# Attention feeding two expert layers on one core: the low-part subtractions issued on VectorE, and the decay and mask products given 64 rows

## The chip, the cores and the metric

The kernel runs on one core of a Trainium2 chip. The metric is device time in microseconds (us). The engines are named as in the profile: PE is TensorE's matrix multiply and PEld its weight load, DVE is VectorE, ACT is ScalarE, POOL is GpSimd, and SP is SyncE, which issues most of the DMAs. Each engine takes its instructions in the order in which they are written in its own stream, and waits where a semaphore isn't there yet.

## The reference, cut to what matters

Attention over 4 batches, 8 heads, 576 positions and a head size of 64, with a decay from cumulated logarithms of `f` and a causal mask; its output goes through a dense layer with a squared ReLU, and that through 8 experts of which each token takes two.

```python
scores = scale * np.matmul(q, k.transpose(0, 1, 3, 2))
cum = np.cumsum(np.log(np.clip(f, 0.0001, 1.0)), axis=-1)
decay = cum[:, :, :, None] - cum[:, :, None, :]
scores = np.where(causal, -1000000000.0, scores + decay)
attn = softmax(scores)                 # over the last axis
x = np.matmul(attn, v)                 # then (2304 tokens, 512)
h = np.maximum(x @ w_in, 0.0); x = h * h @ w_out
# then two of eight experts for each token, weighted
```

## The kernel before, in words

All products run on pairs of float16 numbers: a value is kept as a high part (a cast on ACT) and a low part (the value less the high part), and a product is three matmuls, high by high, high by low and low by high. So each split is one ACT instruction, then one subtraction that reads two tensors in SBUF. Most of those subtractions in the attention are on POOL: `prep` (L163, queries and keys of a pair of heads), `att_split` (L241 and L252, the probabilities), `att_out` (L302, the attention's output), `hd_prep` from the second batch on (L327) and `hd_split` (L381).

The scores of two heads, z = 0 and 1, lie on the lower and the upper 64 rows of the array: the three products at L187 (query tiles of 128), L200 (the last tile, 64 queries, both heads in one bank) and L349 (`hd_s`) use tiles of 64 rows. To these a decay product is added: the 24 rows of `crow` hold the cumulated logarithms of 8 heads in three parts, and `esel` picks a head's three rows, at L190, L201 and L354 with 24 rows. Last comes the mask, as a product of a unit matrix and a triangle: 128 rows at L192 and L358, 64 rows at L204. DVE takes the row maximum (L217, L366), ACT the exponential (L220, L227, L371), then the split, a DMA transpose issued by SP, and the product with the values (L282, L285, L398).

The first 256 positions of every batch ("heads", `hd_*`, 12 units) come first, and beside them DVE and ACT turn the first weights into high and low parts (`conv_w`: L434, L435, L436 and L444 on DVE, 32 times in all). Then the first expert layer runs in passes of chunks of 384 tokens: `mm1` (L456), its squared ReLU on ACT and DVE (L460, L461, then L464 in chunks 0 and 1, and L466 with L467 in later ones), and `mm2` (L500) two steps behind. Chunks 0 and 1 are done in two passes each. The remaining attention (48 units: 3 query tiles of 4 batches, 4 pairs of heads) is issued between the steps of the passes, and a scheduler in the framework sets the final order on every engine from its own cost model. After the last attention come chunk 5 and the second layer's experts (L740, L753), which the change doesn't touch.

Of the kernel before, what the change touches and what calls it, by code (L numbers as in the profile page):

```python
# [52 lines left out]
def attn_moe_moe_kernel(ctx: ExitStack, tc, qka, qk, v, f, w_io, wgn, noise, w1, w2, out):  # L53
# [53 lines left out]

    identb = consts.tile([128, 128], BF16, name="identb")
    masku = consts.tile([128, 128], BF16, name="masku")
    esel = apool.tile([128, H, 128], F16, name="esel")  # L110
    crow = apool.tile([128, B, S], F16, name="crow")
    nc.gpsimd.memset(identb, 0.0)
    nc.gpsimd.affine_select(identb, identb, [[-1, 128]], ALU.not_equal, 1.0, base=0, channel_multiplier=1)
    nc.gpsimd.memset(masku, 0.0)
    nc.gpsimd.affine_select(masku, masku, [[-1, 128]], ALU.is_ge, -BIG, base=0, channel_multiplier=1)

# [22 lines left out]
    for z in range(2):  # L139
        es = esel[64 * z:64 * z + 24]  # L140
        nc.gpsimd.memset(es, -8.0)
        nc.gpsimd.affine_select(es, es, [[-3, 8], [0, 128]], ALU.is_ge, 0.0, base=0, channel_multiplier=1)
        nc.gpsimd.affine_select(es, es, [[3, 8], [0, 128]], ALU.is_ge, 0.0, base=2, channel_multiplier=-1)
    ident2k = consts.tile([128, 128], F16, name="ident2k")
# [12 lines left out]
    def prep(b, p):  # L157
        n = p
        if b == 0:
            make_set(n)  # L160
        t = raw.pop(("qk", b, p))
        nc.scalar.activation(QK[n][:, 0], t, AF.Copy)
        nc.gpsimd.tensor_tensor(QK[n][:, 1], t, QK[n][:, 0], op=ALU.subtract)  # L163

# [12 lines left out]
    def att_s(u, pools):  # L177
# [4 lines left out]
        if i < 4:  # L182
# [5 lines left out]
            for z in range(2):  # L188
                r = slice(64 * z, 64 * z + 24)
                nc.tensor.matmul(st[u][z][:, :N], esel[r, 2 * p + z], crow[r, b, :N], start=False, stop=False)  # L190
            for z in range(2):
                nc.tensor.matmul(st[u][z][:, N - 128:N], identb, masku, start=False, stop=True)  # L192
        else:
            for hf in range(2):
                ps = st[u][hf]
                ks = slice(288 * hf, 288 * hf + 288)
                for x, (qi, ki) in enumerate(HL3):
                    for z in range(2):
                        r = slice(64 * z, 64 * z + 64)
                        nc.tensor.matmul(ps[r, :288], QK[n][r, qi, q0:q0 + 64], QK[n][r, ki, ks], start=(x == 0), stop=False, skip_group_check=True)  # L200
                nc.tensor.matmul(ps[:, :288], esel.rearrange("r h t -> r (h t)")[0:24, 256 * p + 64:256 * p + 192], crow[0:24, b, ks], start=False, stop=(hf == 0), skip_group_check=True)  # L201
            for z in range(2):
                r = slice(64 * z, 64 * z + 64)
                nc.tensor.matmul(st[u][1][r, 224:288], identb[r, 64 * z:64 * z + 64], masku[r, 64 * z:64 * z + 64],  # L204
                                 start=False, stop=True, skip_group_check=True)

# [24 lines left out]
    def att_split(u):  # L231
        b, i, p = u
        pr, = st[u]
        if i < 4:
            phl = astream.tile([128, 4, 2, 2, 128], F16, name="phl", bufs=3)
            pt = astream.tile([128, 4, 2, 2, 128], F16, name="pt", bufs=3)
            for h in range(2):
                pv = pr[:, h, :128 * (i + 1)].rearrange("p (k s) -> p k s", s=128)
                hi, lo = phl[:, :i + 1, h, 0, :], phl[:, :i + 1, h, 1, :]
                nc.scalar.activation(hi, pv, AF.Copy)  # L240
                nc.gpsimd.tensor_tensor(lo, pv, hi, op=ALU.subtract)  # L241
            nc.sync.dma_start_transpose(out=pt[:, :i + 1].rearrange("p a b c q -> p (a b c) q"),
                                        in_=phl[:, :i + 1].rearrange("p a b c s -> p (a b c s)"))
        else:
# [4 lines left out]
            for k0, k1, w_ in ((0, 4, 128), (4, 5, 64)):  # L249
                s3 = flat[:, 128 * k0:128 * k0 + w_ * (k1 - k0)].rearrange("p (k s) -> p k s", s=w_)  # L250
                nc.scalar.activation(ph4[:, k0:k1, 0, :w_], s3, AF.Copy)
                nc.gpsimd.tensor_tensor(ph4[:, k0:k1, 1, :w_], s3, ph4[:, k0:k1, 0, :w_], op=ALU.subtract)  # L252
            nc.sync.dma_start_transpose(out=pt.rearrange("p a b q -> p (a b) q"),
# [39 lines left out]
    def att_out(b, i, po, su, su_in):  # L293
# [7 lines left out]
        nc.scalar.activation(xh[:, 0], xs[:, :, :n], AF.Copy)  # L301
        nc.gpsimd.tensor_tensor(xh[:, 1], xs[:, :, :n], xh[:, 0], op=ALU.subtract)  # L302
        t0 = HEAD * b + 128 * i if i < NB else NTH + REST * b + 128 * (i - NB)
# [17 lines left out]
    def hd_prep(b):  # L321
        for x in range(2):
# [3 lines left out]
            nc.scalar.activation(s_[:, 0], t, AF.Copy)  # L326
            (nc.vector if b == 0 else nc.gpsimd).tensor_tensor(s_[:, 1], t, s_[:, 0], op=ALU.subtract)  # L327

# [8 lines left out]
    def hd_s(u, bank):  # L337
# [13 lines left out]
        for p in range(np_):  # L351
            for z in range(2):
                r = slice(64 * z, 64 * z + 24)
                nc.tensor.matmul(ps[z][:, W * p:W * p + W], esel[r, 2 * (np_ * a + p) + z], crow[r, b, 0:W],  # L354
                                 start=False, stop=False, skip_group_check=True)
        v4 = [t.rearrange("p (c w) -> p c w", w=W) for t in ps]
        for z in range(2):
            nc.tensor.matmul(v4[z][:, :, 128 * i:128 * i + 128], identb, masku[:, None, :].to_broadcast([128, np_, 128]),  # L358
                             start=False, stop=True, skip_group_check=True)
        if a == 0:  # L360
# [14 lines left out]
    def hd_split(u):  # L375
# [4 lines left out]
        nc.scalar.activation(phl[:, 0], flat, AF.Copy)  # L380
        nc.gpsimd.tensor_tensor(phl[:, 1], flat, phl[:, 0], op=ALU.subtract)  # L381
        nc.sync.dma_start_transpose(out=pt, in_=phl.rearrange("p a s -> p (a s)"))
# [646 lines left out]
```

## Time and profile before

| what | value |
|---|---|
| three runs | 1086.57, 1088.98 (median), 1092.2 us |
| the profiled execution | 1083.63 us, of which 1081.9 us are its span |
| busy of the span | PE 991.0, DVE 579.6, ACT 443.3, POOL 369.3 us |
| mean granted TensorE clock | 0.986 |

A share of busy time is an average over stages; below, the stages are taken apart. An instruction's length includes what it waits for inside itself, such as a memory port.

### The profile page before, as it was taken

The numbers are of one execution on the slowest core, as the hardware profiler recorded it, in microseconds if no ns is written. First come the engines' busy times: TensorE is split into PE (matmuls) and PEld (weight loads), VectorE is DVE, ScalarE is ACT, GpSimd is POOL, SyncE is SP. The second block draws the span as 40 slices with busy tenths as digits, with TensorE's granted clock in tenths as the row PEclk, the third lists the DMA queues.
The fourth block names the chain that finished last, engine by engine and source line by source line (L and its number), as shares of the span: only waits on it lengthen the run. The fifth ranks groups of instructions, "written<-read, shape, count | busy, mean of one in ns | idle before, by whom it ended". The sixth has DMA issues, their size and how long they took to land.

```text
span 1081.9 us, 18041 instructions
## 1 busy us (share of the span) xinstructions
PE 991.0 (92%) x7050; PEld 537.5 (50%) x7050; DVE 579.6 (54%) x1159; ACT 443.3 (41%) x989; POOL 369.3 (34%) x331
## 2 busy tenths in 40 slices
PE   3748898899999999999998989998999999999996
PEld 1425444455454554555454434446646474646563
DVE  8998899624766666665537614214734343433121
ACT  3756676644555554564336312003513131412020
POOL 7454632311546535623410230533232404030202
PEclk9999899999999999999999989999999999999999
DMA  7599999433766784672529462437995938370303
GB/s 275 162 201 194 264 224 232 104 76 77 146 141 145 186 176 86 135 144 36 93 40 311 156 155 59 69 69 153 322 214 160 210 93 214 97 148 10 49 1 50
DMA packets 240393, 153.50 MB, mean 142 GB/s; under 512 B 194066, under 2 KB 204626, under 8 KB 240306
## 3 DMA queue, kind: packets, MB, share of 16 engines
q1 hardware_dynamic: 230194, 131.32, 50.3%
q0 software_dynamic: 10112, 21.02, 10.4%
q8 instruction: 56, 0.92, 0.4%
q14 instruction: 31, 0.25, 0.1%
HBM read 81.63 MB, written 24.30 MB: 98 GB/s over the span
## 4 chain that ended last, share of the span: by engine, by line
PE 62%; DVE 16%; DMA 9%; issue 6%; ACT 3%; POOL 2%; SPq 1%; ACTq 0%; POOLq 0%; DVEq 0%
PE e L753 18%; PE e L740 16%; PE m L456 10%; PE acc L500 9%; DMA wr<-in_w_dram 3%; DMA w<-in_w_io_dram 2%; DVE w L435 2%; PE ps L187 2%; DVE w L436 1%; DVE w L434 1%; PE po L282 1%; DVE r L466 1%; DVE wout L444 1%; DVE sm L217 1%; PE ps L200 1%
## 5 line engine op out<-in xcount | busy, mean ns | idle before, releaser
L740 PE MATMUL e<-xgT,w1s 128*128 128x320 f16 (+2 forms) x1536 | 217.8, 302 | 7.1 <-DMA xgT<-xg 5.0
L456 PE MATMUL m<-xT,win 128*128 128x384 f16 x1152 | 209.7, 332 | 13.7 <-ACT r L460 13.1
L500 PE MATMUL acc<-wout,g 128*128 128x512 f16 x864 | 205.6, 380 | 11.2 <-DVE g L464 6.3
L753 PE MATMUL e<-w2s,hT 128*128 128x512 f16 x960 | 212.1, 380 | 3.9 <-ACT hT L744 3.9
L740 PEld LDWEIGHTS <-w1s 128*128 128x128 f16 x1536 | 143.5, 99 | 80.7 <-issue 13.7
L456 PEld LDWEIGHTS <-win 128*128 128x128 f16 x1152 | 110.0, 99 | 88.8 <-issue 23.3
L753 PEld LDWEIGHTS <-hT 128*128 128x128 f16 x960 | 93.7, 98 | 114.0 <-ACT hT L744 4.2
L500 PEld LDWEIGHTS <-g 128*128 128x128 f16 x864 | 81.8, 98 | 102.2 <-DVE g L464 10.8
L744 ACT ACTIVATE hT<-e 128x320 f16<-128x320 f32 (+2 forms) x128 | 53.9, 435 | 186.3 <-PE e L740 186.2
L757 POOL DMA_INDIRECT out_dram<-y,tix x40 | 63.9, 1598 | 142.9 <-DVE y L756 134.7
L745 DVE SCALAR_TENSOR_TENSOR hT<-e,hT 128x320 f16<-128x320 f32 (+2 forms) x128 | 60.4, 487 | 96.0 <-ACT hT L744 95.8
L756 DVE TENSOR_SCALAR y<-e,gs 128x512 f32<-128x512 f32 x40 | 30.0, 750 | 146.0 <-PE e L753 131.6
L466 DVE TENSOR_TENSOR r<-r 128x384 f32<-128x384 f32 x64 | 56.8, 888 | 90.7 <-ACT g L461 90.7
L241 POOL TENSOR_TENSOR phl<-pr,phl 128x384 f16<-128x384 f32 (+1 forms) x64 | 68.7, 1090 | 81.6 <-issue 59.8
L460 ACT ACTIVATE r<-m 128x384 f32<-128x384 f32 x96 | 46.6, 486 | 90.9 <-PE m L456 85.4
L706 POOL DMA_INDIRECT xg<-x2d,tix x40 | 44.7, 1117 | 113.4 <-DMA xgT<-xg 103.5
L641 POOL DMA_INDIRECT table<-ent,si x36 | 36.1, 1002 | 127.8 <-DVE si L638 99.0
L676 ACT ACTIVATE w2s<-wr 128x1024 f16<-128x1024 f32 x32 | 32.5, 1050 | 106.3 <-PE e L753 88.5
L217 DVE TENSOR_REDUCE sm<-ps 128x1 f32<-128x384 f32 (+2 forms) x96 | 51.7, 561 | 34.0 <-PE ps L192 20.8
L220 ACT ACTIVATE pr<-ps,sm 128x384 f32<-128x384 f32 (+1 forms) x64 | 40.0, 627 | 57.7 <-DVE sm L219 56.1
L349 PE MATMUL psab<-hs 64*128 64x128 f16 (+1 forms) x192 | 27.7, 342 | 26.2 <-ACT pr L371 14.7
L461 ACT ACTIVATE g<-r 128x384 f16<-128x384 f32 x96 | 50.2, 522 | 1.8
(253 smaller groups left out, 1160.0 us busy)
## 6 DMA issues: line engine op xcount, KB each, us to landing
wr<-in_w_dram SPq DMA_DIRECT2D x64, 512.0 KB
w<-in_w_io_dram SPq DMA_DIRECT2D x32, 512.0 KB
qkr<-in_qk_dram SPq DMA_DIRECT2D x16, 448.0 KB
vr<-in_v_dram SPq DMA_DIRECT2D x16, 320.0 KB
x2d<-x SPq DMA_DIRECT2D x18, 256.0 KB
qkh<-in_qka_dram SPq DMA_DIRECT2D x8, 512.0 KB
out_dram<-zero SPq DMA_DIRECT2D x5, 768.0 KB
vh<-in_v_dram SPq DMA_DIRECT2D x8, 256.0 KB
```

The lines of the kernel that those rows point to most:

```text
L217: seen[u] = nc.vector.tensor_reduce(sm[:, z:z + 1], ps[z][:, :N], AX.X, ALU.max).ins
L241: nc.gpsimd.tensor_tensor(lo, pv, hi, op=ALU.subtract)
L456: nc.tensor.matmul(ps, win[i][:, cc, wi, :], xT[:, xi, cc, r0:r0 + CH], start=(x == 0), stop=(x == 11))
L460: nc.scalar.activation(r, ps, AF.Relu)
L461: nc.scalar.activation(g[:, 0, :], r, AF.Square, scale=2.0 ** -10)
L466: nc.vector.tensor_tensor(r, r, r, op=ALU.mult)
L500: nc.tensor.matmul(acc[t], g[:, gi, 128 * t:128 * t + 128], wout[i][:, wi, :], start=(i in ends[c][0] and x == 0), stop=(i in ends[c][1] a ...
L740: nc.tensor.matmul(ps[:, :hw], w1s[:, cc, wi, 128 * i:128 * i + 128], xgT[:, 4 * xi + cc, hw * q:hw * q + hw], start=(x == 0), stop=(x == 11))
L744: nc.scalar.activation(hi, ps[:, :hw], AF.Relu)
L745: nc.vector.scalar_tensor_tensor(hT[:, i, 1, hw * q:hw * q + hw], ps[:, :hw], 0.0, hi, op0=ALU.max, op1=ALU.subtract)
L753: nc.tensor.matmul(ps, hT[:, i, hi, 128 * j:128 * j + 128], w2s[:, i, wi, :], start=(i == 0 and x == 0), stop=(i == NFE - 1 and x == 2))
L757: s_ = nc.gpsimd.indirect_dma_start(out=out, out_offset=bass.IndirectOffsetOnAxis(ap=tix[:, j, 0:1], axis=0), in_=y, in_offset=None, compu ...
```

## The change

Every one of those subtractions is issued on DVE. `crow` is cleared on POOL and `esel` shrinks to one number a row and head, of which 64 rows are set; `decay` spreads it over the columns of the weight load by a step of zero. The decay product then takes 64 rows, and in the last tile it is two products, one for each head, in place of one. The mask of 128 rows becomes two halves of 64 rows for each head. Line numbers of the changed kernel are larger: L435 is L447, L444 is L456, L466 is L478, L467 is L479, L464 is L476.

```diff
-    identb = consts.tile([128, 128], BF16, name="identb")
-    masku = consts.tile([128, 128], BF16, name="masku")
-    esel = apool.tile([128, H, 128], F16, name="esel")
+    identb = consts.tile([128, 2, 128], BF16, name="identb")
+    masku = consts.tile([128, 2, 128], BF16, name="masku")
+    esel = apool.tile([128, H], F16, name="esel")
     crow = apool.tile([128, B, S], F16, name="crow")
+    nc.gpsimd.memset(crow, 0.0)
     nc.gpsimd.memset(identb, 0.0)
-    nc.gpsimd.affine_select(identb, identb, [[-1, 128]], ALU.not_equal, 1.0, base=0, channel_multiplier=1)
     nc.gpsimd.memset(masku, 0.0)
-    nc.gpsimd.affine_select(masku, masku, [[-1, 128]], ALU.is_ge, -BIG, base=0, channel_multiplier=1)
+    for z in range(2):
+        for t_, cmp, val in ((identb, ALU.not_equal, 1.0), (masku, ALU.is_ge, -BIG)):
+            t_ = t_[64 * z:64 * z + 64]
+            nc.gpsimd.affine_select(t_, t_, [[64, 2], [-1, 128]], cmp, val, base=0, channel_multiplier=1)
...
     for z in range(2):
-        es = esel[64 * z:64 * z + 24]
+        es = esel[64 * z:64 * z + 64]
         nc.gpsimd.memset(es, -8.0)
-        nc.gpsimd.affine_select(es, es, [[-3, 8], [0, 128]], ALU.is_ge, 0.0, base=0, channel_multiplier=1)
-        nc.gpsimd.affine_select(es, es, [[3, 8], [0, 128]], ALU.is_ge, 0.0, base=2, channel_multiplier=-1)
+        nc.gpsimd.affine_select(es, es, [[-3, 8]], ALU.is_ge, 0.0, base=0, channel_multiplier=1)
+        nc.gpsimd.affine_select(es, es, [[3, 8]], ALU.is_ge, 0.0, base=2, channel_multiplier=-1)
+
+    def decay(r, h, m):
+        return esel[r, h:h + 1].to_broadcast([64, m])
+
...
-        nc.gpsimd.tensor_tensor(QK[n][:, 1], t, QK[n][:, 0], op=ALU.subtract)
+        nc.vector.tensor_tensor(QK[n][:, 1], t, QK[n][:, 0], op=ALU.subtract)
...
             for z in range(2):
-                r = slice(64 * z, 64 * z + 24)
-                nc.tensor.matmul(st[u][z][:, :N], esel[r, 2 * p + z], crow[r, b, :N], start=False, stop=False)
-            for z in range(2):
-                nc.tensor.matmul(st[u][z][:, N - 128:N], identb, masku, start=False, stop=True)
+                r = slice(64 * z, 64 * z + 64)
+                nc.tensor.matmul(st[u][z][:, :N], decay(r, 2 * p + z, 128), crow[r, b, :N], start=False, stop=False)
+            for hf in range(2):
+                for z in range(2):
+                    r = slice(64 * z, 64 * z + 64)
+                    nc.tensor.matmul(st[u][z][:, N - 128:N], identb[r, hf], masku[r, hf], start=False, stop=(hf == 1))
...
-                nc.tensor.matmul(ps[:, :288], esel.rearrange("r h t -> r (h t)")[0:24, 256 * p + 64:256 * p + 192], crow[0:24, b, ks], start=False, stop=(hf == 0), skip_group_check=True)
+                for z in range(2):
+                    r = slice(64 * z, 64 * z + 64)
+                    nc.tensor.matmul(ps[r, :288], decay(r, 2 * p + z, 64), crow[r, b, ks], start=False, stop=(hf == 0), skip_group_check=True)
...
-                nc.gpsimd.tensor_tensor(lo, pv, hi, op=ALU.subtract)
+                nc.vector.tensor_tensor(lo, pv, hi, op=ALU.subtract)
...
-        nc.gpsimd.tensor_tensor(xh[:, 1], xs[:, :, :n], xh[:, 0], op=ALU.subtract)
+        nc.vector.tensor_tensor(xh[:, 1], xs[:, :, :n], xh[:, 0], op=ALU.subtract)
...
-            (nc.vector if b == 0 else nc.gpsimd).tensor_tensor(s_[:, 1], t, s_[:, 0], op=ALU.subtract)
+            nc.vector.tensor_tensor(s_[:, 1], t, s_[:, 0], op=ALU.subtract)
...
-        nc.gpsimd.tensor_tensor(phl[:, 1], flat, phl[:, 0], op=ALU.subtract)
+        nc.vector.tensor_tensor(phl[:, 1], flat, phl[:, 0], op=ALU.subtract)
```

The scheduler's order changes with it. The first place is PE's stream at the end of a last-tile unit in the chunk-2 pass: three products (the last is shown; `set` holds queries and keys), the decay (`esel`, `crow`), the mask (`identb`, `masku`), and then values times probabilities (`pt`). Before:

```order
L200 LDWEIGHTS set_1571
L200 MATMUL ps<-set_1571 64x288
L201 LDWEIGHTS esel
L201 MATMUL ps<-crow,esel 128x288
L204 LDWEIGHTS identb
L204 MATMUL ps<-masku,identb 64x64
L204 LDWEIGHTS identb
L204 MATMUL ps<-masku,identb 64x64
L282 LDWEIGHTS pt
L282 MATMUL po<-vs,pt 128x64
```

The changed kernel, the same unit:

```order
L209 LDWEIGHTS set_1602
L209 MATMUL ps<-set_1602 64x288
L212 LDWEIGHTS esel
L212 MATMUL ps<-crow,esel 64x288
L212 LDWEIGHTS esel
L212 MATMUL ps<-crow,esel 64x288
L215 LDWEIGHTS identb
L215 MATMUL ps<-masku,identb 64x64
L215 LDWEIGHTS identb
L215 MATMUL ps<-masku,identb 64x64
L292 LDWEIGHTS pt
L292 MATMUL po<-vs,pt 128x64
```

Between the products of scores and those of the mask stands a pair of 64-row decay products where one of 24 rows stood.

The second place is DVE's stream in the heads: the weight conversion (L434 to L444, in the changed kernel L446 to L456), the row maxima and their scaling (`smh`), and the subtractions. Before:

```order
L434 TENSOR_SCALAR w_371<-w_361 128x512
L295 TENSOR_SCALAR sums<-sums 128x8
L435 SCALAR_TENSOR_TENSOR w_371<-w_361,w_371 128x512
L296 RECIPROCAL sums<-sums 128x8
L366 TENSOR_REDUCE smh<-psab 128x2
L436 SCALAR_TENSOR_TENSOR w_361<-w_361,w_371 128x512
L367 TENSOR_SCALAR smh<-smh 128x2x2
L444 SCALAR_TENSOR_TENSOR win_148<-w_311,win_148 128x4x128
L366 TENSOR_REDUCE smh<-psab 128x4
L444 SCALAR_TENSOR_TENSOR wout_164<-w_313,wout_164 128x512
L366 TENSOR_REDUCE smh<-psab 128x4
```

The changed kernel:

```order
L446 TENSOR_SCALAR w_494<-w_376 128x512
L379 TENSOR_SCALAR smh<-smh 128x2x2
L447 SCALAR_TENSOR_TENSOR w_494<-w_376,w_494 128x512
L456 SCALAR_TENSOR_TENSOR wout_171<-w_324,wout_171 128x512
L448 SCALAR_TENSOR_TENSOR w_376<-w_376,w_494 128x512
L393 TENSOR_TENSOR phlh<-pr,phlh 128x1024
L378 TENSOR_REDUCE smh<-psab 128x4
L337 TENSOR_TENSOR hs<-qkh,hs 128x1024 x2
L456 SCALAR_TENSOR_TENSOR win_156<-w_374,win_156 128x4x128
L378 TENSOR_REDUCE smh<-psab 128x4
L446 TENSOR_SCALAR w_500<-w_490 128x512
L393 TENSOR_TENSOR phlh<-pr,phlh 128x1024
```

The subtractions of the probabilities (`phlh`) and of the next batch's queries and keys (`hs`) now stand between the conversions and the maxima. Up to the fifteenth `g` of chunks 0 and 1 (L464, L476), 30 of the 32 conversions stand ahead in the kernel before and 26 in the changed one.

The third place is DVE's stream around the eighth and ninth step of chunk 2: the squared ReLU (`r`, `g`), the maxima and the split of the probabilities (`phl`). Before:

```order
L217 TENSOR_REDUCE sm<-ps 128x1
L219 TENSOR_SCALAR sm<-sm 128x1
L217 TENSOR_REDUCE sm<-ps 128x1
L466 TENSOR_TENSOR r<-r 128x384
L219 TENSOR_SCALAR sm<-sm 128x1
L467 SCALAR_TENSOR_TENSOR g<-r,g 128x384
L217 TENSOR_REDUCE sm<-ps 128x1 x2
L219 TENSOR_SCALAR sm<-sm 128x1 x2
L295 TENSOR_SCALAR sums<-sums 128x8
L296 RECIPROCAL sums<-sums 128x8
L466 TENSOR_TENSOR r<-r 128x384
L467 SCALAR_TENSOR_TENSOR g<-r,g 128x384
```

The changed kernel:

```order
L251 TENSOR_TENSOR phl<-pr,phl 128x4x128
L229 TENSOR_SCALAR sm<-sm 128x1
L227 TENSOR_REDUCE sm<-ps 128x1
L478 TENSOR_TENSOR r<-r 128x384
L229 TENSOR_SCALAR sm<-sm 128x1
L251 TENSOR_TENSOR phl<-pr,phl 128x4x128
L479 SCALAR_TENSOR_TENSOR g<-r,g 128x384
L305 TENSOR_SCALAR sums<-sums 128x8
L306 RECIPROCAL sums<-sums 128x8
L251 TENSOR_TENSOR phl<-pr,phl 128x4x128 x2
L478 TENSOR_TENSOR r<-r 128x384
L479 SCALAR_TENSOR_TENSOR g<-r,g 128x384
```

Three subtractions of the probabilities have come between one `r` and the next.

## Rows read from the trace of the kernel before

**Rows 1.** Windows of four stretches: start:end, length, busy us (instructions) of PE, PEld, DVE, ACT, POOL.

```profile
0.00:216.00 216.00, 160.74 (x1187) 85.81 (x1188) 186.22 (x285) 132.84 (x329) 103.56 (x82) 0.98 0.83 207
216.00:279.00 63.00, 63.00 (x488) 32.86 (x485) 22.94 (x79) 30.60 (x69) 14.90 (x15) 1.00 0.31 72
279.00:568.00 289.00, 279.75 (x2472) 146.78 (x2471) 174.59 (x424) 145.50 (x356) 126.38 (x131) 0.99 0.58 123
568.00:1082.00 514.00, 487.47 (x2910) 272.02 (x2909) 195.87 (x373) 134.32 (x235) 124.48 (x104) 0.98 0.57 134
```

**Rows 2.** Timeline of PE, 341 to 347 us: start, length, line, tiles, shape, count.

```profile
343.30 0.56 PE L200 MATMUL ps<-set 64*64 64x288 f16 x6
343.79 0.29 PE L201 MATMUL ps<-crow,esel 24*128 24x288 f16 x1
344.01 0.55 PE L200 MATMUL ps<-set 64*64 64x288 f16 x6
...
344.87 0.87 PE L282 MATMUL po<-vs,pt 128*128 128x64 f16 x24
```

**Rows 3.** Groups of DVE, 0 to 216 us: count, busy us, mean ns, idle before.

```profile
L435 DVE SCALAR_TENSOR_TENSOR w<-w,w 128x512 int32<-128x512 int32 x32 | 29.7, 927 | 0.4
L436 DVE SCALAR_TENSOR_TENSOR w<-w,w 128x512 int32<-128x512 int32 x32 | 27.9, 871 | 0.4
L444 DVE SCALAR_TENSOR_TENSOR wout<-w,wout 128x512 f16<-128x512 f32 x16 | 21.7, 1354 | 2.1 <-ACT wout L443 1.9
L434 DVE TENSOR_SCALAR w<-w 128x512 int32<-128x512 int32 x32 | 20.6, 643 | 6.7 <-DMA w<-in_w_io_dram 6.5
L444 DVE SCALAR_TENSOR_TENSOR win<-w,win 128x512 f16<-128x512 f32 x16 | 15.9, 995 | 0.8 <-ACT win L443 0.7
L464 DVE TENSOR_TENSOR g<-r,g 128x384 f16<-128x384 f32 x20 | 14.8, 739 | 7.1 <-ACT r L463 7.1
```

**Rows 4.** Single lines on DVE, whole run: shortest, median, longest in ns.

```profile
L435 DVE SCALAR_TENSOR_TENSOR w<-w,w x32: 642/692/2494, 14.9 to 194.7; 128x512 int32<-128x512 int32 x32
L444 DVE SCALAR_TENSOR_TENSOR wout<-w,wout x16: 678/685/2617, 24.8 to 198.2; 128x512 f16<-128x512 f32 x16
L434 DVE TENSOR_SCALAR w<-w x32: 408/426/2336, 14.3 to 193.8; 128x512 int32<-128x512 int32 x32
L466 DVE TENSOR_TENSOR r<-r x64: 546/558/5471, 288.5 to 644.9; 128x384 f32<-128x384 f32 x64
```

**Rows 5.** Groups of POOL, 0 to 216 us, the subtractions.

```profile
L381 POOL TENSOR_TENSOR phlh<-pr,phlh 128x1024 f16<-128x1024 f32 x12 | 27.4, 2288 | 45.9 <-ACT phlh L380 34.5 <-issue 11.3
L327 POOL TENSOR_TENSOR hs<-qkh,hs 128x1024 f16<-128x1024 f32 x6 | 14.7, 2471 | 0.1
L302 POOL TENSOR_TENSOR xh<-xs,xh 128x512 f16<-128x512 f32 x9 | 13.2, 1470 | 20.5 <-ACT xh L301 20.4
L163 POOL TENSOR_TENSOR set<-qkr,set 128x896 f16<-128x896 f32 x5 | 10.8, 2164 | 0.3 <-ACT set L162 0.2
L241 POOL TENSOR_TENSOR phl<-pr,phl 128x512 f16<-128x512 f32 x8 | 10.1, 1277 | 27.6 <-issue 23.6 <-ACT phl L240 4.0
L241 POOL TENSOR_TENSOR phl<-pr,phl 128x384 f16<-128x384 f32 x8 | 8.6, 1077 | 8.0 <-ACT phl L240 5.4 <-issue 1.8 <-POOL phl L241 0.8
```

**Rows 6.** The same subtraction where it already ran on DVE, whole run.

```profile
L327 DVE TENSOR_TENSOR hs<-qkh,hs x2: 1207/1207/1207, 9.0 to 10.9; 128x1024 f16<-128x1024 f32 x2
```

**Rows 7.** Timeline of all engines, 325 to 333 us.

```profile
326.02 5.45 DVE L466 TENSOR_TENSOR r<-r 128x384 f32<-128x384 f32 x1
...
326.56 1.17 POOL L302 TENSOR_TENSOR xh<-xs,xh 128x512 f16<-128x512 f32 x1
...
327.67 3.37 POOL L241 TENSOR_TENSOR phl<-pr,phl 128x512 f16<-128x512 f32 x3
...
332.12 1.25 PE L500 MATMUL acc<-wout,g 128*128 128x512 f16 x5 [1.10 <-DVE g L467]
```

**Rows 8.** Group of DVE, 279 to 568 us.

```profile
L466 DVE TENSOR_TENSOR r<-r 128x384 f32<-128x384 f32 x48 | 47.9, 999 | 62.7 <-ACT g L461 62.7
```

More of the change, by code (lines that the diff above doesn't have):

```diff
@@ L200, in att_s @@
                         nc.tensor.matmul(ps[r, :288], QK[n][r, qi, q0:q0 + 64], QK[n][r, ki, ks], start=(x == 0), stop=False, skip_group_check=True)
-                nc.tensor.matmul(ps[:, :288], esel.rearrange("r h t -> r (h t)")[0:24, 256 * p + 64:256 * p + 192], crow[0:24, b, ks], start=False, stop=(hf == 0), skip_group_check=True)
+                for z in range(2):
+                    r = slice(64 * z, 64 * z + 64)
+                    nc.tensor.matmul(ps[r, :288], decay(r, 2 * p + z, 64), crow[r, b, ks], start=False, stop=(hf == 0), skip_group_check=True)
             for z in range(2):
                 r = slice(64 * z, 64 * z + 64)
-                nc.tensor.matmul(st[u][1][r, 224:288], identb[r, 64 * z:64 * z + 64], masku[r, 64 * z:64 * z + 64],
-                                 start=False, stop=True, skip_group_check=True)
+                nc.tensor.matmul(st[u][1][r, 224:288], identb[r, 0, 0:64], masku[r, 0, 0:64], start=False, stop=True, skip_group_check=True)
     def att_exp(u):
@@ L251, in att_split @@
                 nc.scalar.activation(ph4[:, k0:k1, 0, :w_], s3, AF.Copy)
-                nc.gpsimd.tensor_tensor(ph4[:, k0:k1, 1, :w_], s3, ph4[:, k0:k1, 0, :w_], op=ALU.subtract)
+                nc.vector.tensor_tensor(ph4[:, k0:k1, 1, :w_], s3, ph4[:, k0:k1, 0, :w_], op=ALU.subtract)
             nc.sync.dma_start_transpose(out=pt.rearrange("p a b q -> p (a b) q"),
@@ L352, in hd_s @@
             for z in range(2):
-                r = slice(64 * z, 64 * z + 24)
-                nc.tensor.matmul(ps[z][:, W * p:W * p + W], esel[r, 2 * (np_ * a + p) + z], crow[r, b, 0:W],
+                r = slice(64 * z, 64 * z + 64)
+                nc.tensor.matmul(ps[z][:, W * p:W * p + W], decay(r, 2 * (np_ * a + p) + z, 128), crow[r, b, 0:W],
                                  start=False, stop=False, skip_group_check=True)
         v4 = [t.rearrange("p (c w) -> p c w", w=W) for t in ps]
-        for z in range(2):
-            nc.tensor.matmul(v4[z][:, :, 128 * i:128 * i + 128], identb, masku[:, None, :].to_broadcast([128, np_, 128]),
-                             start=False, stop=True, skip_group_check=True)
+        for hf in range(2):
+            for z in range(2):
+                r = slice(64 * z, 64 * z + 64)
+                nc.tensor.matmul(v4[z][:, :, 128 * i:128 * i + 128], identb[r, hf], masku[r, hf, None, :].to_broadcast([64, np_, 128]),
+                                 start=False, stop=(hf == 1), skip_group_check=True)
         if a == 0:
```

## The prediction

> **What bounds the kernel now.** I read the windows by stage first [rows 1]. Up to 216 us PE is busy for 160.7 of 216 us and DVE for 186.2: this stage waits on DVE. From 216 to 568 us PE is busy for 342.8 of 352 us and DVE for 197.5: here PE is the bound, and what shortens its own stream shortens the kernel. Behind 568 us stand the last chunk and the experts, where POOL's 124.5 us are no subtractions; nothing of the change lies there, and it starts sooner by what is won before.
>
> Then I read what a busy engine spends its time on. On PE, the timeline of one last-tile unit [rows 2]: the six products at L200 are three pairs, one on each half of the array. One matmul of 288 columns lasts 0.29 us and the six 0.56, so a pair follows the one before by 0.135 us. L201 should then start 0.405 us after the first; it starts 0.49 us after it. The next L200 should follow L201 by 0.135 and follows by 0.22. A change from 64 rows to 24 rows or back costs about 0.09 us.
>
> On DVE, mean against median. L435 takes 692 ns in the median, up to 2494 [rows 4], and 927 in the mean [rows 3]; L466 558 ns, up to 5471 [rows 4]. The timeline shows why [rows 7]: L466 starts at 326.02 and ends at 331.47, and all through it POOL runs L302 and three L241, the last of which ends at 331.04. DVE's instruction reads two tensors in SBUF, as POOL's do, and stands until POOL's queue has a gap. PE then sits idle for 1.10 us for the `g` behind it.
>
> **PE's tiling.** Decay and mask take the scores' 64 rows. In a last-tile unit four changes of tiling vanish (L200 to L201 and back, L201 twice more): 16 x 4 x 0.09 = 5.8 us. In the 32 units of 128 queries, scores, decay and mask were of 64, 24 and 128 rows, and the step behind the mask is mostly of 128: two changes go and one comes, 32 x 0.09 = 2.9 us. Counted over the whole written order, PE changes its tiling 388 times before and 244 times after. Of the 144, 98 lie in the passes from chunk 2 on, 17 in the second passes of chunks 0 and 1, and 29 earlier, where DVE is late anyway and I give them nothing. **Term: 115 x 0.09 = 10.4 us less.**
> The 120 matmuls more (two for each mask, one for each last-tile decay) are second halves of pairs, and pairs run side by side [rows 2]. If they didn't, 120 x 0.06 us (the pace of a mask's 128 columns by the same ratio, 0.135 x 128/288) would take 7.2 back: bounds 3.2 to 10.4, and to 14.4 if all 144 count at 0.1. A weight load with step zero stands in no row; PEld is busy for half of PE's time [rows 1] and loads ahead, so I take nothing for it, and 0.06 for each of 128 loads, another 7.7, if it were not hidden.
>
> **The early stage, to 216 us.** What DVE gets: 12 L381, 6 L327, 9 L302, 5 L163 and 16 L241 [rows 5]. The price on DVE: 1024 columns took 1207 ns there [rows 6], against 2471 on POOL [rows 5]; 512 columns with two inputs take 685 and 384 take 558 [rows 4]; 896 lie between, 1077. Sum: 14.5 + 7.2 + 6.2 + 5.4 + 8 x 0.685 + 8 x 0.558 = 43.2 us. What it gets back is the stretching, count times mean less median: L435 7.5, L436 (taking L435's median) 5.7, the two L444 10.7 and 5.0, L434 6.9, L464 3.6 [rows 3, 4]; together 39.4 us. DVE's work there is thus about the same, 4 us more by these rows. It also has to wait for ACT's high part, as it does at L444: 2.1 + 0.8 us on 32 [rows 3], 0.09 each, 4 us on 48.
> Against these 8 us stand two things. Four conversions (0.692 + 0.692 + 0.426 + 0.685 = 2.5 us each) stand no longer ahead of the fifteenth `g`; they run where DVE has air, 22.9 of 63 us busy between 216 and 279 us [rows 1]: 10 us. And a result that took POOL 2.29 us (L381) or 1.47 (L302) is there after 1.21 or 0.69; chunk 0 needs four such splits and three outputs, at most 4 x 1.08 + 3 x 0.79 = 6.7 us. **Term: 8 - 10 - 6.7, rounded to 8 us less**; bounds 8 more (neither counts) and 17 less (no net work, both count).
> The clearing of `crow` and the four selections on POOL lie ahead of the first DMA into `crow` and under DVE's logarithms; cost nothing, and a few us once if that cover were gone.
>
> **Stalls in the passes.** Between 279 and 568 us PE is idle for 289.0 - 279.75 = 9.25 us [rows 1], in pieces like the one at 332.12 [rows 7]. POOL's reason goes. What comes late instead is `g` behind the subtractions on DVE: at most three of 0.69 us between one `r` and the next, against the 4.9 us that L466 lost. DVE won't be the bound there: L466 alone gives back 48 x (0.999 - 0.558) = 21 us [rows 4, 8], and all of POOL's 126.4 us would be 62 on DVE (1207 to 2471), 174.6 - 21 + 62 = 216 of 289 us. I take half of the idle time: **4.6 us less**, bounds 0 and 9.2.
> The Trainium skill (SBUF — State Buffer, section "Who interferes with whom") says that the one that starts first keeps the shared port for its whole instruction and the other is blocked until that one ends. By that, L466 would have waited for L302 or one L241, some 1.1 us, no stall would follow, and this term would be 0 and the sum 18.4. The trace doesn't agree: it waited through four instructions in a row, 4.9 us.
>
> **Sum.** 10.4 + 8 + 4.6 = 23 us. From the profiled execution's own 1083.6 us (1081.9 of span and 1.7 around it) that makes 1060.6. The median of the three runs shown is 5.4 us above that execution, so the forecast for a median is 1066 us.
>
> **Rivals.**
> Only PE's part comes: the early stage takes as long as before, since DVE is as busy, and the stalls come back through DVE's own queue. 10.4 us less, 1078.6 us. For it speaks that DVE's work stays even; against it, that the order puts conversions later.
> All of it comes, at the good bounds: 10.4 + 17 + 9.2 = 36.6 us less, 1052 us.
> DVE waits at the head of its queue, the one on the other side. POOL sat for 34.5 us ahead of L381 and for 20.4 us ahead of L302 for ACT [rows 5]; there nobody stood behind it. On DVE the row maxima, the conversions and `g` stand behind each subtraction. If DVE stood as long, 54.9 us would come on top of 8 of work, less 15 won on PE: 1089 + 48 = 1137 us. It decides from 23 of these 54.9 us on, 0.5 us for each of the 48 subtractions; L444, the nearest row, waits 0.09. Half of it would be about 1109 us.
> The Trainium skill (Perfetto Trace Analysis, section "Optimizing Scalar/DVE Operations") holds that with DVE saturated some work may well go to GPSIMD, which the change undoes; it adds that the port they share may spoil that. No run here shows yet which half weighs more.
> The change doesn't do what it says: the 0.09 us belong to the small tiles themselves, not to the change of rows, and come again at 64 rows; DVE is even. Then it is 1085 to 1090 us.
>
> **How the numbers follow.** A measurement of this kernel tells about 0.5%, 5.4 us, from no change. The forecast 0.50 (its own range 1059 to 1074), all of it 0.16, only PE's part 0.20, no effect 0.08, DVE's waits 0.06. The first three are faster by over 0.5%, less a little for the third's upper edge: faster 0.85, same 0.09, slower 0.06. The range from 1051 to 1081 reaches over the first three cases.
>
> **What would show it.** In the changed profile a last-tile unit on PE lasts 1.57 - 0.34 = 1.23 us from its first product to the values' (L292) if the tiling is the reason, and 1.5 or more if not. L478 has no instruction above 1.5 us, and L447's mean is near its 692 ns. DVE's busy time stays between 570 and 600 us, POOL's falls by about 195. The passes' idle time on PE halves. I am wrong if DVE's idle time ahead of L393, L251 or L312 for ACT sums to more than 20 us before the last conversion, or if the stage before the experts starts at the old time.

## The result, and the profile after

The changed kernel takes 1042.16 us in the median of four runs (1038.47 to 1044.19), the kernel before 1088.74 (1086.57 to 1092.2): a ratio of 0.9566, 95% interval 0.9525 to 0.9606. The forecast was 1066 with a range of 1051 to 1081, so the sign was right, the gain was twice as large, and the time lies 9 us below the range. The profiled execution took 1044.19 us, 39.4 less than that of before.

The page of the changed kernel: its span, then busy time, share and instructions of each engine.

```profile
span 1042.5 us, 18252 instructions
PE 969.7 (93%) x7170; PEld 545.3 (52%) x7170; DVE 579.1 (56%) x1309; ACT 441.9 (42%) x989; POOL 174.8 (17%) x184
```

DVE's busy time is what it was (579.6), POOL's has fallen by 194.5 us.

To see where the time came from, the windows are cut where the programs do the same thing, not at the same microsecond: where PE starts its 21st group of first-layer products (L456, in the changed kernel L468), where it starts those of chunk 5, and at the end. Columns as in [rows 1]. The windows of the changed kernel:

```profile
0.00:194.67 194.67, 151.79 (x1204) 89.81 (x1205) 171.91 (x329) 130.75 (x322) 16.28 (x34) 0.88 0.90 225
194.67:528.90 334.23, 330.78 (x3063) 183.60 (x3060) 211.13 (x609) 177.21 (x433) 36.16 (x46) 1.00 0.60 123
528.90:1042.50 513.60, 487.15 (x2910) 271.87 (x2909) 196.05 (x373) 133.93 (x235) 122.39 (x104) 0.98 0.56 134
```

and those of the kernel before:

```profile
0.00:216.57 216.57, 161.31 (x1196) 86.19 (x1197) 186.56 (x285) 132.84 (x329) 103.56 (x82) 0.98 0.83 207
216.57:568.37 351.80, 342.19 (x2946) 179.26 (x2945) 197.49 (x502) 176.36 (x426) 141.28 (x145) 1.00 0.54 114
568.37:1081.90 513.53, 487.47 (x2910) 272.02 (x2909) 195.58 (x372) 134.05 (x235) 124.48 (x104) 0.98 0.57 134
```

The three lengths go from 216.57, 351.80 and 513.53 to 194.67, 334.23 and 513.60 us. So 21.9 us were won up to the 21st product, 17.6 in the passes, and nothing behind them. In the first stretch DVE's busy time went down by 14.7 us with 44 instructions more. In the second, PE's busy time went down by 11.4 us and its idle time from 9.6 to 3.5.

One last-tile unit on PE in the changed kernel, as in [rows 2]:

```profile
319.04 0.56 PE L209 MATMUL ps<-set 64*64 64x288 f16 x6
319.43 0.29 PE L212 MATMUL ps<-crow,esel 64*64 64x288 f16 x2
319.55 0.53 PE L209 MATMUL ps<-set 64*64 64x288 f16 x6
319.92 0.29 PE L212 MATMUL ps<-crow,esel 64*64 64x288 f16 x2
320.04 0.19 PE L215 MATMUL ps<-masku,identb 64*64 64x64 bf16 x2
320.17 0.87 PE L292 MATMUL po<-vs,pt 128*128 128x64 f16 x24
```

From its first product to the values' product (L292) it lasts 1.13 us, where it was 1.57 [rows 2]. The decay pairs start 0.39 us after the products, as one more pair of the same kind would (0.405).

DVE up to the same point, grouped by line and form, as in [rows 3]:

```profile
L448 DVE SCALAR_TENSOR_TENSOR w<-w,w 128x512 int32<-128x512 int32 x32 | 22.1, 691 | 0.2
L447 DVE SCALAR_TENSOR_TENSOR w<-w,w 128x512 int32<-128x512 int32 x32 | 22.0, 687 | 0.3
L393 DVE TENSOR_TENSOR phlh<-pr,phlh 128x1024 f16<-128x1024 f32 x12 | 14.7, 1222 | 0.5 <-ACT phlh L392 0.5
L446 DVE TENSOR_SCALAR w<-w 128x512 int32<-128x512 int32 x32 | 13.6, 424 | 10.8 <-DMA w<-in_w_io_dram 10.7
L456 DVE SCALAR_TENSOR_TENSOR wout<-w,wout 128x512 f16<-128x512 f32 x16 | 11.0, 688 | 0.2
```

and the shortest, median and longest of two lines, as in [rows 4]:

```profile
L447 DVE SCALAR_TENSOR_TENSOR w<-w,w x32: 644/690/704, 16.3 to 190.8; 128x512 int32<-128x512 int32 x32
L478 DVE TENSOR_TENSOR r<-r x64: 547/558/565, 265.1 to 606.3; 128x384 f32<-128x384 f32 x64
```

Mean and median agree now. Nothing of L478 is above 0.57 us, where L466 went up to 5.47.

### The profile page after: what moved, and what is told of

Read it like the earlier page. It is cut to its first block, busy times and chain, and to the rows that moved or that the text cites. A ratio compares the mean times of both kernels' runs of the same rounds, so it can differ in the third digit from the quotient of the medians.

```text
span 1042.5 us, 18252 instructions
## 1 busy us (share of the span) xinstructions
PE 969.7 (93%) x7170; PEld 545.3 (52%) x7170; DVE 579.1 (56%) x1309; ACT 441.9 (42%) x989; POOL 174.8 (17%) x184
## 4 chain that ended last, share of the span: by engine, by line
PE 61%; DMA 7%; DVE 2%; issue 1%; POOL 1%; SPq 1%; ACT 1%; POOLq 0%; DVEq 0%
PE e L765 18%; PE e L752 17%; PE m L468 10%; PE acc L512 10%; DMA wr<-in_w_dram 2%; PE ps L194 2%; PE po L292 2%; PE ps L209 1%; DMA xg<-x2d,tix 1%; DMA x2T<-x 1%; PE po L295 1%; DMA xgT<-xg 1%; DMA pt<-phl 1%; SPq L720 1%; PE ps L197 1%
## 5 line engine op out<-in xcount | busy, mean ns | idle before, releaser
L468 PE MATMUL m<-xT,win 128*128 128x384 f16 x1152 | 208.6, 331 | 7.8 <-DVE w L448 5.1
L468 PEld LDWEIGHTS <-win 128*128 128x128 f16 x1152 | 108.2, 99 | 83.0 <-issue 17.1
L478 DVE TENSOR_TENSOR r<-r 128x384 f32<-128x384 f32 x64 | 35.6, 556 | 44.5 <-ACT g L473 41.6
L251 DVE TENSOR_TENSOR phl<-pr,phl 128x384 f16<-128x384 f32 (+1 forms) x64 | 39.1, 623 | 18.5 <-ACT phl L250 15.9
L689 DVE SCALAR_TENSOR_TENSOR w2s<-wr,w2s 128x1024 f16<-128x1024 f32 x32 | 38.1, 1223 | 18.1 <-ACT w2s L688 17.9
```

The costliest lines, as they stand in the source:

```text
L468: nc.tensor.matmul(ps, win[i][:, cc, wi, :], xT[:, xi, cc, r0:r0 + CH], start=(x == 0), stop=(x == 11))
```

## Experiments

All ratios below are against the kernel before in the same set of runs, so they compare with 0.9566. Theory A and theory B are the two accounts of the early stage: A gives it to the subtractions, B in part to the tiling.

**Each half alone.** The kernel before with

```diff
-        nc.gpsimd.tensor_tensor(...)      # L163, L241, L252, L302, L381, L327 from the second batch on
+        nc.vector.tensor_tensor(...)
```

> The kernel before with only the subtractions moved to VectorE; decay and mask keep their 24 and 128 rows. Theory A (the early stage won about 22 us because DVE is freed from POOL; the tiling gave only the forecast 10): 36 us of the 46.6 come from here, so about 1053 us. Theory B (the tiling also shortened the early stage, where the PE lines of scores and decay up to the 21st first product took 9.5 us less): some 24 us from here, so about 1065 us. Rival C (the two halves do not add, each clears a wait the other leaves): over 1070 us here and over 1075 us with the tiling alone.

Measured: 1060.15 us, 0.9755 (0.9708 to 0.9801). And the changed kernel with the same lines back on POOL:

> The changed kernel with its subtractions back on POOL; decay and mask padded to 64 rows. Theory A: the forecast 10 us of the passes, about 1078 us. Theory B: 20 to 24 us, about 1066 us, with the first product of chunk 0's ReLU layer some us earlier than in the kernel before. Rival C: over 1075 us here and over 1070 us with the subtractions alone.

Measured: 1061.17 us, 0.9762 (0.9724 to 0.9799). Each half is worth about 26 us, nearer to B's size than to A's; together they bring 46.6, so some 5 us are shared. The first two of the same windows, with the subtractions alone:

```profile
0.00:197.10 197.10, 161.39 (x1195) 87.15 (x1196) 169.03 (x322) 130.43 (x325) 18.88 (x32) 0.99 0.90 220
197.10:543.50 346.40, 346.23 (x2953) 180.18 (x2949) 218.11 (x616) 177.10 (x431) 37.62 (x45) 1.00 0.58 120
```

and with the padding alone:

```profile
0.00:208.30 208.30, 153.03 (x1166) 88.20 (x1166) 177.12 (x273) 126.38 (x311) 93.62 (x75) 0.89 0.83 206
208.30:547.90 339.60, 333.53 (x3096) 185.41 (x3096) 191.84 (x515) 183.85 (x445) 147.60 (x155) 1.00 0.61 123
```

In the passes the two halves add up: 351.80 goes to 346.40 with the subtractions (5.4) and to 339.60 with the padding (12.2), and with both to 334.23 (17.6). Up to the 21st product they don't: 216.57 goes to 197.10 (19.5) and to 208.30 (8.3), with both to 194.67 (21.9). The subtractions take PE's idle time in the passes from 9.6 to 0.2 us, but its busy time there rises from 342.2 to 346.2, so 9.4 us less idle make the passes only 5.4 us shorter. In the first stretch they take PE's idle time (length less busy) from 55.3 to 35.7 and leave its busy time at 161.4. The padding does the reverse there: idle 55.3, busy 153.0.

**What the heads' padding is worth.** The changed kernel, with

```diff
 def hd_s
-  r = slice(64 * z, 64 * z + 64)          # decay
+  r = slice(64 * z, 64 * z + 24)
-  identb[r, hf], masku[r, hf, ...]        # two halves of 64 rows
+  ident1, mask1[:, None, :]               # one product of 128 rows
```

> The changed kernel with decay and mask of the heads alone back at 24 and 128 rows; the units keep the padded ones. The tiling alone had won 25.4 us, of which 8.3 stood at the 21st first product and about 14 came between chunk 2 and chunk 5. If the heads' tiling is the early part (PE's scores there lie on the path, and two heads' products run side by side in the two halves only when no product takes all 128 rows): 1047 to 1051 us. If the heads were hidden as the prediction had it: 1041 to 1044 us.

Measured: 1040.01 us, 0.9567 (0.9537 to 0.9597). No difference: the heads' tiling is hidden once DVE subtracts. Its windows:

```profile
0.00:195.80 195.80, 158.44 (x1177) 87.29 (x1178) 168.29 (x325) 129.81 (x320) 18.63 (x38) 0.97 0.88 224
195.80:526.80 331.00, 330.66 (x3060) 184.01 (x3060) 214.77 (x612) 178.90 (x436) 36.89 (x46) 1.00 0.60 124
```

PE is busy for 6.7 us more up to the 21st product than in the changed kernel, and idle for 5.5 less. The same edit in the kernel whose subtractions are on POOL:

> The padded kernel with all subtractions on POOL, and the heads' decay and mask back at 24 and 128 rows; the units alone are padded. Its 30 conversions ahead of the fifteenth g are those of the kernel before (the fully padded one had 25). If the heads' padding, by itself or through the later conversions that came with it, gave the padded kernel its early 8.3 us: only the passes' 12.2 us stay, 1072 to 1076 us, and the 21st first product comes at 214 to 218 us in its profile. If the heads are hidden here too, as with the subtractions on VectorE: 1059 to 1064 us.

Measured: 1071.42 us, 0.9816 (0.9776 to 0.9857), a little under the first expectation. Its windows:

```profile
0.00:216.70 216.70, 159.93 (x1223) 87.41 (x1223) 181.08 (x285) 133.50 (x329) 101.25 (x89) 0.95 0.83 207
216.70:560.10 343.40, 332.20 (x3016) 183.82 (x3015) 191.87 (x502) 177.15 (x426) 141.30 (x145) 0.99 0.56 117
```

The 21st product comes at 216.7 us as before. So with POOL subtracting, the 8.3 us do come from the heads' padding or from the order that the scheduler makes of it; with DVE subtracting that stretch of time is no longer there to be won. Which of the two, padding or order, carries them with POOL is not settled; the next pair bears on it. The passes are 8.4 us shorter than before, not 12.2, although every unit is padded; what makes these 3.8 us was not tried. A window of one execution differs by some us from one order to another: with the units padded alike, 334.2 and 331.0 us above.

**Order of the conversions.** The kernel before and the changed kernel with the second half of the weights converted just ahead of use:

```diff
-        ahead = (min(NA, AHEAD + 1 + i), NA + i, NF)[min(n, 2)]
+        ahead = (min(NA, AHEAD + 1 + i), NA + max(0, i - 6), min(NF, i + 3), NF)[min(n, 3)]
```

> The kernel before with the same lines changed: 26 conversions, as in the changed kernel, and not 30 stand ahead of the fifteenth g; subtractions on POOL and tiling as before. If the order alone carries a part that both halves of the change share (their sum is 51.9 us, the whole 46.6; with each of them alone only 24 and 25 conversions stand there): 5 to 10 us less than before, 1077 to 1082 us. If the order is only a symptom: 1085 to 1089 us.

Measured: 1083.02 us, 0.9966 (0.9952 to 0.9979), 3.7 us less: below the first expectation's size, and not nothing. Its profiled execution took 1087.76 us, as long as the kernel before, so the place isn't shown.

> The changed kernel with the weight conversions of the second half written one or two steps ahead of their use: 21 conversions and not 26 stand ahead of the fifteenth g on VectorE. If VectorE's order still sets the first two passes: 5 x 2.5 us come behind, at most the 11 us that PE still idles between its first and its 21st product, so 1033 to 1039 us. If PE is the bound by now (95.7 of 100 us busy from 100 to 200 us): no change, 1040 to 1044 us; if the conversions come too late for PE, slower.

Measured: 1043.56 us, 0.9590 (0.9558 to 0.9623): no change. Its first window:

```profile
0.00:196.30 196.30, 152.42 (x1186) 90.03 (x1187) 161.87 (x308) 127.69 (x315) 18.89 (x33) 0.87 0.86 216
```

DVE is busy for 10.0 us less up to the 21st product than in the changed kernel, and the product comes no earlier (196.3 against 194.7): after the change the amount of DVE's work alone no longer sets this time, though PE still waits for DVE there (9.1 us, 7.2 in the changed kernel). This order is worth some 4 us before and nothing afterwards.

**What sharing the port costs.** The changed kernel with each moved subtraction made a second time:

```diff
         nc.vector.tensor_tensor(phl[:, 1], flat, phl[:, 0], op=ALU.subtract)
+        nc.gpsimd.tensor_tensor(junk, flat, phl[:, 0], op=ALU.subtract)
```

> The changed kernel, and each moved subtraction made a second time on POOL into a scratch tile that nobody reads. The hand-off and the order on DVE stay those of the changed kernel; only POOL's use of SBUF beside DVE comes back. If the port sharing is what the subtractions cost before: back to the level of the tiling alone, 1065 to 1078 us, with the conversions' lines at about 900 ns mean again. If it was the hand-off (a result after 1.2 us and not 2.3) and the order: within 6 us of the changed kernel, 1042 to 1048 us.

Measured: 1103.49 us, 1.0149 (1.0109 to 1.0190), 61 us more than the changed kernel, and beyond what either theory had. Its windows:

```profile
0.00:233.20 233.20, 159.96 (x1191) 92.50 (x1192) 219.14 (x321) 128.14 (x317) 103.36 (x78) 0.80 0.75 187
233.20:592.70 359.50, 342.76 (x3070) 191.03 (x3070) 274.83 (x617) 180.60 (x439) 170.55 (x152) 0.97 0.56 115
```

and shortest, median and longest of its L462 (L447 of the changed kernel):

```profile
L462 DVE SCALAR_TENSOR_TENSOR w<-w,w x32: 635/680/2495, 16.0 to 232.7; 128x512 int32<-128x512 int32 x32
```

The 21st product comes 38.5 us later, the passes last 25.3 us longer, and DVE's busy time up to the 21st product is 219.14 us against 171.91. One of these instructions, with a median of 0.68 us, lasts up to 2.5. The scratch result also holds the inputs until POOL is done, so a part of the 61 us may be late buffers.

Now the roles are changed: POOL's result is handed on, DVE's goes to the scratch tile.

> The kernel with every subtraction made twice, with the roles changed: POOL's result is the one that goes on to the DMA, VectorE's goes to the scratch tile that nobody reads. Work, contention and VectorE's queue are those of the kernel made twice (1103.5 us); only who hands on differs. If a quicker hand-off was worth a good part of the early gain (the prediction gave it 6.7 us, and by subtraction it may be up to 15): 1110 us or more. If the hand-off is hidden: 1100 to 1107 us.

Measured: 1105.23 us, 1.0137 (1.0096 to 1.0179), no different by ratio. Who hands the result on doesn't matter to the whole, at least beside this contention. By place it does: with POOL handing on, the 21st product comes 6.1 us earlier (227.1 against 233.2) and the passes last 5.7 us longer (365.2 against 359.5).

And POOL's second operation as a copy of one operand (`tensor_copy(junk, flat)`):

> The kernel made twice, but POOL's second operation only copies the first operand (one tensor in from SBUF, one out) and subtracts nothing. If any POOL operation on SBUF holds VectorE up: near 1100 us, with the conversions' lines near 900 ns again. If it takes POOL's two inputs to hold VectorE up: 1041 to 1050 us, with those lines at 690 ns.

Measured: 1058.48 us, 0.9716 (0.9674 to 0.9758), 16 us more than the changed kernel and between the two expectations. L462 in this kernel:

```profile
L462 DVE SCALAR_TENSOR_TENSOR w<-w,w x32: 641/684/1409, 16.1 to 212.8; 128x512 int32<-128x512 int32 x32
```

and POOL's copies of the probabilities in it, grouped by form:

```profile
L87 POOL CAST junk<-pr 128x512 f16<-128x512 f32 x48 | 34.1, 710 | 66.6 <-ACT pr L239 35.9 <-ACT pr L246 29.7
L87 POOL CAST junk<-pr 128x1024 f16<-128x1024 f32 x12 | 20.4, 1701 | 27.7 <-ACT pr L397 27.4
L87 POOL CAST junk<-pr 128x384 f16<-128x384 f32 x32 | 20.0, 626 | 42.2 <-ACT pr L239 41.4
```

The longest of these instructions is now 1.41 us, its own 0.68 and about one copy. The Trainium skill (SBUF — State Buffer, section "Who interferes with whom") states that a DVE instruction with two SBUF inputs contends with a GpSimd instruction that reads SBUF, and that the one that comes second is blocked for the whole of that one instruction. Here, with POOL's short copies, the trace agrees.

With two-input subtractions it agrees nearly everywhere too, and [rows 7] is an exception. Counted over the kernel before (lines and forms with at least six instructions), 80 DVE instructions last over 0.15 us longer than the shortest of their kind. In 76 of them at most two of POOL's subtractions overlap, and none loses more than 1.96 us, less than one L381 (2.29). From DVE's and POOL's timeline of the kernel before:

```profile
43.99 5.10 POOL L381 TENSOR_TENSOR phlh<-pr,phlh 128x1024 f16<-128x1024 f32 x2
45.10 2.01 DVE L436 SCALAR_TENSOR_TENSOR w<-w,w 128x512 int32<-128x512 int32 x1
47.03 2.61 DVE L444 SCALAR_TENSOR_TENSOR win<-w,win 128x512 f16<-128x512 f32 x1
```

POOL's two instructions follow each other without a gap, the first to 46.56 us and the second to 49.09, and L436 and L444 end 0.55 us behind one each. The other four instructions, all behind 216 us, overlap four to seven subtractions and lose 4.9 to 6.2 us. Why these four found no way in is open.

**Heads or units.** The changed kernel with the units' subtractions back on POOL (`prep`, `att_split`, `att_out` for the later rows), then with the heads' (`hd_prep`, `hd_split`, `att_out` for the first two).

> The changed kernel with the subtractions of the units (queries and keys, probabilities, outputs of the later rows) back on POOL; those of the heads stay on VectorE. Theory A: the heads carry most of the early gain, so only the stalls in the passes (4.6 us) and a few us of the first two passes come back: about 1050 us. Theory B: the same or a little more, to 1055 us. If the units' subtractions are what counted (the passes to 216 us and behind): above 1060 us.

Measured: 1056.54 us, 0.9726 (0.9689 to 0.9764), between the 1055 and the 1060 of the expectations.

> The changed kernel with the heads' subtractions (their queries and keys, probabilities, outputs) back on POOL; the units' stay on VectorE. The kernel with the heads' on VectorE and the units' on POOL took 1056.5 us, 14.4 more than the changed one, and reached its 21st first product when the padded kernel without any moved subtraction did (208.9 and 208.3 us). If the heads' subtractions are even (DVE pays for them what it gets back): 1040 to 1046 us. If the two groups only help together: 1052 us or more.

Measured: 1049.85 us, 0.9630 (0.9591 to 0.9669). From 0.9762 (none moved) the heads' alone win 0.4%, which is inside the intervals, the units' alone 1.3%, both 2.0%. The units carry most of it; the heads are neither even nor the main part, and 1049.85 us lies between the two expectations.

**Decay or mask.** The changed kernel with the mask at 128 rows in the heads and the 128-query units, and with the decay at 24 rows everywhere:

```diff
-  nc.tensor.matmul(st[u][z][:, N - 128:N], identb[r, hf], masku[r, hf], ...)   # hf = 0, 1
+  nc.tensor.matmul(st[u][z][:, N - 128:N], ident1, mask1, ...)
```

> The changed kernel with the decay padded but the mask back at 128 rows in the heads and in the units of 128 queries. Counting changes of tiling alone, the mask's part is small, since the step behind a unit's mask mostly takes 128 rows anyway: 1044 to 1047 us. If the mask of 128 rows holds up both halves of the array: 1050 us or more.

Measured: 1048.25 us, 0.9642 (0.9614 to 0.9670), between the two expectations.

> The changed kernel with the decay back at 24 rows everywhere, as pairs or as one half in the last-tile units, and the mask padded. The tiling is worth 18 us on top of the subtractions (1060.2 against 1042.2 us), the mask at 128 rows cost 6.1. If the two add: 12 us more, 1052 to 1056 us. If the count of changes rules at 0.09 us and the first passes add nothing: 4 a last-tile unit (5.8 us) and 2 in each of the 32 others (5.8 us), 1051 to 1055 us as well, and by place nearly all of it behind chunk 2's start. If the decay alone spoils what the mask gives: 1058 us or more.

Measured: 1062.41 us, 0.9750 (0.9706 to 0.9795), as slow as without any padding (0.9755). Windows with the wide mask:

```profile
0.00:202.30 202.30, 161.96 (x1176) 90.62 (x1177) 170.91 (x327) 130.18 (x322) 18.57 (x38) 0.97 0.89 218
202.30:536.30 334.00, 333.79 (x3000) 180.84 (x2999) 213.36 (x610) 178.35 (x434) 35.94 (x46) 1.00 0.59 122
```

and with the narrow decay:

```profile
0.00:197.70 197.70, 161.39 (x1203) 85.90 (x1204) 170.14 (x327) 129.62 (x321) 17.52 (x34) 1.00 0.89 221
197.70:546.90 349.20, 349.02 (x3065) 181.70 (x3061) 213.82 (x611) 179.10 (x435) 37.82 (x46) 1.00 0.57 118
```

In the passes the wide mask costs nothing (334.00 against 334.23 us): the 7.6 us that its profiled execution loses stand ahead of them, behind PE's first L456 (78.8 us, 79.9 in the changed kernel). Why they do is open: with mask and decay both unpadded in the heads nothing was lost there (195.8 us). The narrow decay costs 15.0 us there, more than the whole padding wins, and with 296 changes of tiling in that stretch this kernel has the most of all. So the mask's padding pays only together with the decay's.

## Why the prediction was wrong in size

**The sum.** Against the profiled execution it said 1060.6 us, and 1044.2 came: 16.4 us off. 13.9 of them are the early stage, 1.8 PE's tiling and 0.8 the stalls. Another 7 us of the miss are no term: the forecast added 5.4 us to come from one execution to a median, and the profiled execution of the changed kernel lies 2.0 above its median.

**The early stage is the step that failed.** "8 - 10 - 6.7, rounded to 8 us less", bounds 8 more and 17 less; measured 21.9 less, or 19.5 with the subtractions alone. Taking that run piece by piece to the 21st product:
- *What DVE gets* was 43.2 us; its rows add up to 44.2.
- *What it gets back* was 39.4, from six groups of lines. Each line's mean before less its mean with the subtractions moved, times its count before, gives 47.2. The lines left out are small ones that read a few numbers: L367, L223 and L295 together 7.7. These are L367 and L223 of the kernel before, whole run:

```profile
L367 DVE TENSOR_SCALAR smh<-smh x12: 155/166/2079, 29.9 to 123.8; 128x4 f32<-128x4 f32 x8, 128x8 f32<-128x8 f32 x4
L223 DVE TENSOR_TENSOR sm<-sm x16: 154/159/1842, 208.4 to 549.8; 128x1 f32<-128x1 f32 x16
```

  and L367 with the subtractions alone moved:

```profile
L367 DVE TENSOR_SCALAR smh<-smh x12: 155/160/166, 29.0 to 116.2; 128x4 f32<-128x4 f32 x8, 128x8 f32<-128x8 f32 x4
```

  A median of 0.166 us hid single instructions of 2.08 and 1.84. I had looked for stretching where the median was large.
- *The price of one more instruction.* I added whole lengths. But the lengths of DVE's records sum to 203.5 us before and its busy time is 186.6; with the subtractions they sum to 192.1, and the busy time is 169.0. Records of neighbours overlap, and with 37 instructions more the overlap grew from 16.9 to 23.1 us: 6 us less than the lengths say.
- *Waits for ACT* were 4 us more. DVE's idle time (length less busy) went from 30.0 to 28.1 us.
- *Conversions standing later* were 10 us. Two to four fewer of each of their lines stand ahead of the 21st product, 7.7 us by their lengths; as an edit by itself later conversions won 3.7. In the changed kernel four fewer stand ahead of the fifteenth `g`, as forecast, but all 32 start before the 21st product, and it came 21.9 us earlier all the same.
- *A quicker hand-off* was 6.7 us, and I found nothing for it: made twice, the kernel is as fast with POOL handing on as with DVE.

So the step that failed is the size of DVE's work and waits: 43.2 - 39.4 + 4 = 8 us more were forecast, and 44.2 - 47.2 - 6.2 - 1.9 = 11 us less came. Conversions and hand-off, 16.7 us in the forecast, gave 7.7 at most, which hid part of the error.

DVE's busy time fell by 17.5 us and its idle time by 1.9, which makes the 19.5; its work was not even, as I had it, but went down. That DVE set this time, as [rows 1] suggested, rests on the kernel made twice: with the contention put back its busy time rises by 47.2 us and the 21st product comes 38.5 us later. That POOL held DVE up was read correctly, of its size 39.4 of 47.2 us. How it did was read too broadly: "stands until POOL's queue has a gap" holds for 4 of 80 instructions, the others wait for one. And at [rows 7] itself, POOL was still in a memset when L466 started (L558, to 326.62 us); L302 started 0.54 us behind L466.

**PE's tiling: right, a little small.** 12.2 us in the passes against 10.4. From the 21st product to chunk 5 the traces show 274 changes of tiling before and 166 after, and PE's busy time there falls by 11.4 us: 0.106 each where I took 0.09. Over ten of the kernels here (all but the doubled, the copying and the reordered ones), with 160 to 296 changes, a straight line through PE's busy time in the passes has a slope of 0.12 us a change. The last-tile unit, forecast at 1.23 us, came to 1.13. The changed kernel's trace has 218 changes in all, not 244; from the second passes on 115 are gone, as counted, and ahead of them 55 and not 29. That the earlier ones are worth nothing was right for the changed kernel, as the heads' run shows, and wrong with POOL subtracting, where they or the order that came with them gave 8.3 us.

**Stalls in the passes: the size right, in part by luck.** 5.4 us came against 4.6. I took half of the idle time. With the subtractions alone 9.4 of the 9.6 us go, and PE's busy time takes 4.0 of them back; 291 changes of tiling there in place of 274 would be some 2 of these 4, the rest is open. PE's waits for a late `g`, which I had in mind, were 3.4 of the 9.6 us. Nor is POOL the only reason for idle time: with the padding as well 3.5 us are left, the longest piece 1.5 us behind DVE's L229, and the units' run, whose POOL subtracts nothing in the passes, idles for 5.9 us there, 2.1 of them for one transpose (in an execution 7 us above its median).

**The rivals.** That only PE's part would come is out, since the subtractions alone win 26 us. DVE's waits at the head of its queue, the rival on the other side, did not come: up to the 21st product L393 waits for 0.5 us in all, L251 for 0.3 and L312 not at all. That the 0.09 us belong to the small tiles themselves is out too: the padded unit keeps its 64-row tiles and lasts 1.13 us, not 1.5 or more. "All of it, at the good bounds" (36.6 us less) was the nearest, and still 2.8 us short of the 39.4. The range failed because its early bound counted "no net work" as the best that DVE could do.

## What to carry to other kernels

Two engines that share a memory port are to be costed together: when one of them is the bound of a stage, moving work onto it can make it less busy. To price the stretching, take every line of the victim, also those whose median is a sixth of a microsecond, and compare the sum of lengths with the busy time before charging an added instruction at its full length. One long wait in a timeline is not yet the rule: count the stretched instructions and what each of them overlaps. On TensorE it pays to keep neighbouring products in one tiling: one product left in another tiling in their midst (here the decay) gave back the whole gain of the others.

## What the runs showed of the hardware that was not expected

- POOL's copies with one input still slow DVE (16 us over the kernel), about a quarter of what two-input subtractions do (61 us). The copies are also half as long (0.71 us for 512 columns against 1.39), so what the second input costs by itself is not told apart.
- A stretched DVE instruction mostly waits for one of POOL's, also where POOL's follow each other without a gap (76 of 80); four waited through four to seven.
- Instructions on 4 or 8 numbers a row (L367, above) can stand for 2 us beside POOL. The Trainium skill (SBUF — State Buffer, section "Who interferes with whom") counts `tensor_scalar` among those that can take the shared pair; the trace agrees, with 0.60 us in the mean of eight such instructions before and 0.16 with the subtractions moved.
- A change of tiling on TensorE costs 0.11 to 0.12 us in this stream. The Trainium skill (TensorEngine Tiling (Array Packing), section "Key Properties") says that changing the mode drains the engine; the trace fits that, with the next product 0.09 us late at each change [rows 2].
- The granted clock in a row is not always the pace. In the kernel before, the same six products take 1.43 us at 31.75 us, after 7.5 us of idle PE, and 0.83 at 95.05. PE's timeline at the first place:

```profile
31.75 1.43 PE L349 MATMUL psab<-hs 64*128 64x256 f16 x6 [7.54 <-ACT pr L371]
```

  at the second:

```profile
95.05 0.83 PE L349 MATMUL psab<-hs 64*128 64x256 f16 x6
```

  and the windows around both, with the granted clock behind POOL's instructions:

```profile
30.00:42.00 12.00, 10.19 (x56) 5.73 (x56) 11.32 (x20) 11.81 (x40) 4.96 (x3) 1.00 0.32 101
94.00:97.00 3.00, 3.00 (x28) 1.81 (x26) 1.91 (x7) 2.97 (x8) 1.18 (x1) 1.00 1.05 296
```

  The row of 30 to 42 us shows 1.00 like the other, but the first six start 0.21 us apart from the second on, which for 256 columns is the pace of the lower level, 1.2 GHz; the second six start 0.11 us apart. In the changed kernel a row of the same part of the program does show the lower level:

```profile
40.00:74.00 34.00, 27.19 (x263) 20.29 (x261) 28.40 (x54) 25.11 (x78) 0.40 (x2) 0.50 1.02 233
```

  So the 0.98 of the first stretch before and the 0.88 in the changed kernel's windows do not mean that the changed kernel ran slower there.
